# Eight key blocks in one score product, one K buffer refilled in place, and weights parked in one part

## The chip, the cores and the metric

The kernel runs on one core of one Trainium2 chip. TensorE multiplies matrices, VectorE, ScalarE and GpSimd work elementwise, and SyncE (SP) issues most of the DMAs. In the profile's rows they are PE (and PEld for its weight loads), DVE, ACT, POOL and SP. The metric is the device time of one execution in microseconds; lower is better. The median over the runs of the kernel before is compared with that of the changed kernel.

## The reference

A block-sparse attention over 4 batches, 8 heads, 768 positions and 64 dimensions a head, whose output goes through a feed-forward layer with a softplus. In blocks of 32 positions there are 24 blocks. A block of queries sees its neighbours (itself and one on each side), the first and the last block, and three sampled blocks; the first and the last block of queries see all keys.

```python
scores = scale * np.matmul(q, k.transpose(0, 1, 3, 2))
mask = np.abs(blk_i - blk_j) <= 1
mask = mask | (blk_i == 0) | (blk_j == 0) | (blk_i == n_blocks - 1) | (blk_j == n_blocks - 1)
for qb in range(n_blocks):
    for kb in sampled_blocks[qb]:
        mask[qb * block:(qb + 1) * block, kb * block:(kb + 1) * block] = True
scores = np.where(mask, scores, -1000000000.0)
attn = softmax(scores)                       # written out with max, exp, sum
x = (attn @ v) as 3072 tokens of 512
h = x @ w_in                                 # 512 -> 2048, weights are float64
g = np.maximum(h, 0.0) + np.log1p(np.exp(-np.abs(h)))
out = (g @ w_out).astype(np.float32)         # 2048 -> 512
```

## The kernel before

Attention goes by *sets*: for each batch six groups `g` of four query blocks (the last one has two, `ni = 2`), and one set `whole` with the first and last query block against all keys, which stands between groups 4 and 5. Each set is two *units* (`a = 0, 1`, four heads each), 56 units in all: 40 with four blocks, 8 with two, 8 whole. A unit passes through `scores`, `exponents`, `transposes`, `values`; `pieces` starts the scores two units ahead of the values.

For a group, `gather_keys` copies keys from `kT`, the keys of a whole batch in SBUF (1.57 MB), into one of two buffers `kg`: three neighbour blocks for each query block in one VectorE copy (L483), and three sampled blocks each by GpSimd with a register as address (L494). `scores` multiplies those six blocks by 16 matmuls of 192 columns (L585) and the two end blocks straight from `kT` by four more (L591); the eight blocks stand side by side in PSUM, and L599 masks them and takes the row minimum. Whole sets multiply with `kT` (L617). `load_kT` fetches the next batch's keys in four parts into the other of two buffers (pools `kv` and `kv2`), spread over earlier pieces. `load_keys` puts a group on the list of keys to be gathered as soon as its batch's `kT` exists.

The feed-forward layer runs over 16 slices `f` of the 2048 hidden columns and over 8 tiles of 384 tokens, three groups each. Phase 0 does slices 0 to 4 (`EARLY`) between the pieces of attention and parks partial sums in DRAM (`yD`), and the attention's output in `xD`; phase 1 does slices 5 to 15 after attention. One step of the loop over `j` is `hidden` (12 matmuls), a softplus on ScalarE and VectorE, and, three steps later (`LEAD`), `project` (9 matmuls). Each float32 product is made of three products of parts: a value rounded to the matmul's type, `hi`, and the rest, `lo`.

`Weights` converts the float64 weights, 32 halves of 128x512 (`which` 0 and 1 for each `f`), in small steps on ScalarE, VectorE and GpSimd (L153 to L193). It ends in `hi` (L189, ScalarE) and `lo` (L193, VectorE). The 22 halves of `f >= 5` are parked in DRAM, both parts (L198, tiles `wh` and `wt`), and come back after attention through `load_w2` (L893).

Every engine's queue runs in the order in which the program issues; SP's order is that of the code.

Of the kernel before, what the change touches and what calls it, by code (L numbers as in the profile page):

```python
# [37 lines left out]
SPREAD = 2  # L38

# [9 lines left out]
def sparse_attention_ffn(  # L49
# [50 lines left out]
    xp = ctx.enter_context(tc.tile_pool(name="x", bufs=2, side="right"))  # L100
# [10 lines left out]
        (which, f): [dram.tile([P, DM], F32, name=f"wD{x}{which}{f}") for x in range(2)]  # L111
# [7 lines left out]
    class Weights:  # L119
# [62 lines left out]
        def high(self, h):  # L182
            f, which = self.halves[h]
            if f < EARLY:
                W[which, f] = [w1.tile([P, DM], F32R, name=f"w{x}{which}{f}") for x in range(2)]
            else:
                hi = pools["conv"].tile([P, DM], F32R, tag="wh", name=f"wh{which}{f}", bufs=2)
                W[which, f] = [hi, self.t[h].bitcast(F32R)]
            tc.keep_in_program_order(nc.scalar.copy(out=W[which, f][0], in_=self.t[h]))  # L189

        def low(self, h):
            hi, lo = W[self.halves[h][::-1]]
            nc.vector.tensor_tensor(out=lo, in0=self.t[h], in1=hi.bitcast(F32), op=ALU.subtract)  # L193

        def park(self, x, h):
            f, which = self.halves[h]
            if f >= EARLY:
                nc.sync.dma_start(out=wD[which, f][x], in_=W[which, f][x].bitcast(F32))  # L198
# [14 lines left out]
        def done(self):  # L213
            return self.at > 4 * (len(self.halves) - 1) + 14
# [6 lines left out]
    def x_tile(phase, t):  # L221
        X[phase, t] = xp.tile([P, 2, NC, TB], F32R, tag="x", name=f"x{phase}_{t}")
# [247 lines left out]

    def gather_keys(m):
# [4 lines left out]
        def of_block(i):  # L476
# [3 lines left out]
            if i == 0:  # L480
# [6 lines left out]
                tc.keep_in_program_order(ins)  # L487
            (r,) = registers(eng, [2 * g + i // 2])
            for s in range(NR):
# [5 lines left out]
                    out=kd[:, i, NR + s, :], in_=kT[b][:, bass.ds(x, 1), :].rearrange("p n f -> p (n f)")  # L495
# [68 lines left out]
    def scores(n):  # L564
# [6 lines left out]
        if not whole:  # L571
# [6 lines left out]
            for j in range(2):  # L578
                p = 2 * a + j
                cols = slice(p * BLOCK, (p + 1) * BLOCK)  # L580
                for i in range(ni):
                    for r in range(2):
                        half = slice(64 * r, 64 * r + 64)
                        o = ps[r][32 * i : 32 * i + 32, j].rearrange("p (c s) k -> p c s k", c=2)[:, :, 0:NR]
                        nc.tensor.matmul(o, qd[half, p, i, :], kd[half, i, :, cols], start=True, stop=True)  # L585

            for j in range(2):
                p = 2 * a + j
                for r in range(2):
                    half = slice(64 * r, 64 * r + 64)  # L590
                    nc.tensor.matmul(  # L591
                        ps[r][rows, j, NR : NS : NR + 1],
                        qd[half, p, 0:ni, :].rearrange("p i q -> p (i q)"),
                        kT[b][half, 0 : NB : LAST, p * BLOCK : (p + 1) * BLOCK],
                        start=True, stop=True,
                    )
# [163 lines left out]
    def pieces(n):  # L760
# [7 lines left out]
        def score_piece():  # L768
# [3 lines left out]
            if s < len(units):  # L772
                scores(s)
                if scored is not None:
                    load_keys(scored + 2)

        def value_piece():
# [10 lines left out]
            b, i = divmod(n, len(units) // B)  # L788
# [71 lines left out]
    kv2 = ExitStack()  # L860
    owed = 0.0

    def convert():
# [5 lines left out]
        while owed >= 1 and not weights.done():  # L869
            weights.tick()  # L870
            owed -= 1
            if weights.at == 4 * weights.extra + 2:
                extractx.close()
                pools["kv2"] = kv2.enter_context(tc.tile_pool(name="kv2", bufs=1))
# [85 lines left out]
```

## Time and profile before

| | |
|---|---|
| median of 3 runs | 853.09 us (847.7 to 854.35) |
| profiled execution | 850.83 us, span 848.8 us |
| TensorE / its weight loads busy | 811.8 us (96%) / 683.7 us (81%) |
| VectorE / ScalarE / GpSimd busy | 582.0 us (69%) / 486.2 us (57%) / 219.4 us (26%) |
| DMA | 142.30 MB, mean 168 GB/s |
| granted TensorE clock, mean | 0.975 |

The span runs from the first to the last instruction; the execution's own time has about 2 us around it. A row of a timeline reads: start in us, duration in us, engine, line, operation, tiles as out<-in, shape, count; in brackets the idle time before it and what ended it. In a group's row stand the number of instructions, the busy time with the mean duration in ns, and the idle time before them with what ended it.

### The profile page before, as it was taken

The numbers are of one execution on the slowest core, as the hardware profiler recorded it, in microseconds if no ns is written. First come the engines' busy times: TensorE is split into PE (matmuls) and PEld (weight loads), VectorE is DVE, ScalarE is ACT, GpSimd is POOL, SyncE is SP. The second block draws the span as 40 slices with busy tenths as digits, with TensorE's granted clock in tenths as the row PEclk, the third lists the DMA queues.
The fourth block names the chain that finished last, engine by engine and source line by source line (L and its number), as shares of the span: only waits on it lengthen the run. The fifth ranks groups of instructions, "written<-read, shape, count | busy, mean of one in ns | idle before, by whom it ended". The sixth has DMA issues, their size and how long they took to land.

```text
span 848.8 us, 22274 instructions
## 1 busy us (share of the span) xinstructions
PE 811.8 (96%) x8492; PEld 683.7 (81%) x8492; DVE 582.0 (69%) x1473; ACT 486.2 (57%) x1167; POOL 219.4 (26%) x389
## 2 busy tenths in 40 slices
PE   8779899999999899999999999999999999999998
PEld 7657677767778677787789999999999999999996
DVE  4587997787888778877655556556565656565564
ACT  3776776667776667666655544444444444444443
POOL 6582855652545625553000000000000000000000
PEclk9797999999999999998999999999999999999999
DMA  8778598686897877965529923112222203030011
GB/s 254 232 216 310 184 238 273 202 281 198 232 304 237 291 234 203 303 192 189 175 82 379 396 87 112 37 75 75 75 75 75 74 26 125 1 124 27 24 52 38
DMA packets 55323, 142.30 MB, mean 168 GB/s; under 512 B 6256, under 2 KB 6384, under 8 KB 53168
## 3 DMA queue, kind: packets, MB, share of 16 engines
q1 hardware_dynamic: 49216, 122.37, 44.2%
q0 software_dynamic: 5712, 17.57, 7.0%
q8 instruction: 67, 1.10, 0.6%
q10 hardware_dynamic: 288, 0.93, 0.3%
q14 instruction: 40, 0.33, 0.1%
HBM read 104.14 MB, written 36.70 MB: 166 GB/s over the span
## 4 chain that ended last, share of the span: by engine, by line
PE 73%; DVE 10%; ACT 9%; DMA 3%; issue 3%; another core or an unknown queue 1%; SPq 0%; DVEq 0%; ACTq 0%
PE o L291 10%; PE o L292 10%; PE o L293 10%; PE h L235 10%; PE h L236 9%; PE h L237 9%; ACT pr L649 5%; PE x L692 4%; PE s L585 4%; PE t L662 3%; PE s L591 2%; DMA vg<-in_v_dram 2%; PE y L737 1%; ACT pt L669 1%; DVE pr L624 1%
## 5 line engine op out<-in xcount | busy, mean ns | idle before, releaser
L235 PE MATMUL h<-x,w 128*128 128x384 f32 x512 | 176.9, 346 | 1.7 <-DVE nmax L624 1.0
L236 PE MATMUL h<-x,w 128*128 128x384 f32 x512 | 173.1, 338 | 0.0
L237 PE MATMUL h<-x,w 128*128 128x384 f32 x512 | 172.5, 337 | 0.0
L246 DVE TENSOR_SCALAR u<-e 128x384 f32<-128x384 f32 x128 | 49.6, 388 | 168.2 <-ACT e L240 168.1
L291 PE MATMUL o<-w,gh 128*128 128x512 f32 x384 | 156.3, 407 | 0.0
L293 PE MATMUL o<-w,gl 128*128 128x512 f32 x384 | 154.1, 401 | 0.0
L292 PE MATMUL o<-w,gh 128*128 128x512 f32 x384 | 153.7, 400 | 0.0
L649 ACT ACTIVATE pr<-pr,nmax 128x256 f32<-128x256 f32 (+2 forms) x208 | 110.3, 532 | 64.7 <-DVE nmax L599 42.3
L239 ACT ACTIVATE e<-h 128x384 f32<-128x384 f32 x128 | 62.8, 490 | 144.0 <-PE h L237 142.1
L263 ACT CAST gh<-u 128x384 fp32r<-128x384 f32 x128 | 65.7, 513 | 80.7 <-PE o L292 80.6
L235 PEld LDWEIGHTS h<-x,w 128*128 128x128 f32 x512 | 96.7, 189 | 10.5 <-DVE nmax L624 3.1
L550 POOL DMA_INDIRECT vg<-in_v_dram,ix x88 | 88.5, 1005 | 60.8 <-PE x L692 31.5
L494 POOL COPY kg<-kT 128x128 f32 x252 | 85.4, 384 | 59.1 <-PE s L585 53.1
L236 PEld LDWEIGHTS h<-x,w 128*128 128x128 f32 x512 | 96.9, 189 | 4.0
L237 PEld LDWEIGHTS h<-x,w 128*128 128x128 f32 x512 | 96.7, 189 | 0.0
L599 DVE CUSTOM_DVE_ANT_1 pr<-s,mask 128x256 f32<-128x256 f32 (+1 forms) x192 | 69.7, 417 | 28.6 <-PE s L591 16.4
L293 PEld LDWEIGHTS o<-w,gl 128*128 128x128 f32 x384 | 73.2, 191 | 17.5
L292 PEld LDWEIGHTS o<-w,gh 128*128 128x128 f32 x384 | 73.3, 191 | 13.5 <-issue 0.6
L291 PEld LDWEIGHTS o<-w,gh 128*128 128x128 f32 x384 | 73.1, 190 | 13.5 <-issue 0.4
L254 ACT ACTIVATE u<-u 128x384 f32<-128x384 f32 x128 | 67.0, 523 | 24.9 <-DVE e L248 24.9
L269 DVE TENSOR_TENSOR gl<-u,gh 128x384 fp32r<-128x384 f32 x128 | 73.7, 576 | 5.6 <-ACT gh L263 5.6
L248 DVE SCALAR_TENSOR_TENSOR e<-u,e 128x384 f32<-128x384 f32 x128 | 73.0, 570 | 3.9
(81 smaller groups left out, 1147.9 us busy)
## 6 DMA issues: line engine op xcount, KB each, us to landing
vg<-in_v_dram SPq DMA_DIRECT2D x19, 768.0 KB
xD<-x SPq DMA_DIRECT2D x8, 1536.0 KB
x<-xD SPq DMA_DIRECT2D x8, 1536.0 KB
w<-wD SPq DMA_DIRECT2D x44, 256.0 KB
raw<-in_w_in_dram SPq DMA_DIRECT2D x16, 512.0 KB
raw<-in_w_out_dram SPq DMA_DIRECT2D x16, 512.0 KB
qc<-in_q_dram SPq DMA_DIRECT2D x24, 256.0 KB
vg<-in_v_dram SPq DMA_DIRECT2D x12, 512.0 KB
```

The lines of the kernel that those rows point to most:

```text
L235: nc.tensor.matmul(ph, wh[:, cols], hi[:, c], start=(c == 0), stop=False)
L236: nc.tensor.matmul(ph, wh[:, cols], lo[:, c], start=False, stop=False)
L237: nc.tensor.matmul(ph, wl[:, cols], hi[:, c], start=False, stop=(c == NC - 1))
L248: nc.vector.scalar_tensor_tensor(out=e, in0=u, scalar=-1.0, in1=e, op0=ALU.add, op1=ALU.subtract)
L269: nc.vector.tensor_tensor(out=gl, in0=l, in1=G[n].bitcast(F32), op=ALU.subtract)
L291: nc.tensor.matmul(po[m], gh[:, cols], wh, start=first, stop=False)
L292: nc.tensor.matmul(po[m], gh[:, cols], wl, start=False, stop=False)
L293: nc.tensor.matmul(po[m], gl[:, cols], wh, start=False, stop=last)
L494: copy(out=kd[:, i, NR + s, :], in_=kT[b][:, bass.ds(x, 1), :].rearrange("p n f -> p (n f)"))
L550: nc.gpsimd.indirect_dma_start(out=vd[0 : 3 * BLOCK, 1, i, :], out_offset=None, in_=v, in_offset=bass.IndirectOffsetOnAxis(ap=ix[:, b, 4 * ...
L599: nc.vector.tensor_tensor_reduce(out=pr[r][rows, j], in0=ps[r][rows, j], in1=mask[rows, g].unsqueeze(2).to_broadcast([ni * BLOCK, NS, BLOCK]),
L649: nc.scalar.activation(x, x, AF.Exp, bias=nmax[rows, r, j : j + 1], scale=-1.0, accum_out=rs[rows, h : h + 1])
```

## The change

Three things are changed together.

1. `kg` gets eight slots for each query block instead of six. `end_keys` copies the first and the last key block into slots 3 and 7, for the first two groups of a batch (the slots are not overwritten by the later groups); on GpSimd, but for the first two groups of the program on VectorE and ScalarE. A unit's scores are then 16 matmuls of 256 columns, and the product straight from `kT` is gone.
2. There is one `kT` buffer. The next batch's four parts are loaded in `score_piece` right behind the scores of the whole set's second unit, the last reader of `kT`, and the gathering of the next batch's first groups is started there. The space of the second buffer goes to one of the two tiles `x` (pool `x2`).
3. A late weight half is parked as the one float32 that `assemble` leaves, eight ticks (`PARK`) after its first step. `high` and `low` are left out for it. `load_w2` loads it into the `lo` tile, and `split_w2` makes the two parts: a ScalarE copy for `hi`, and a GpSimd subtraction in place for `lo`, for two halves a step ahead of their use.

```diff
-    kg = [ac.tile([P, NI, 2 * NR, NP * BLOCK], F32, name=f"kg{n}") for n in range(2)]
+    kg = [ac.tile([P, NI, NS, NP * BLOCK], F32, name=f"kg{n}") for n in range(2)]
...
-            kT[b] = (pools["kv2"] if b % 2 else kv).tile([P, NB, NP * BLOCK], F32, tag="kT", name=f"kT{b}")
+            kT[b] = kv.tile([P, NB, NP * BLOCK], F32, tag="kT", name=f"kT{b}")
...
+    def end_keys(m, copies):
+        for copy, slot, blkno in zip(copies, (NR, 2 * NR + 1), (0, LAST)):
+            copy(
+                out=kg[m % 2][:, :, slot, :],
+                in_=kT[order[m][0]][:, blkno : blkno + 1, :].to_broadcast([P, NI, NP * BLOCK]),
+            )
...
+                if m % NG < 2:
+                    first = nc.vector.tensor_copy if m == 0 else nc.scalar.copy
+                    end_keys(m, (first, nc.scalar.copy) if m < 2 else 2 * (nc.gpsimd.tensor_copy,))
...
-                        o = ps[r][32 * i : 32 * i + 32, j].rearrange("p (c s) k -> p c s k", c=2)[:, :, 0:NR]
-                        nc.tensor.matmul(o, qd[half, p, i, :], kd[half, i, :, cols], start=True, stop=True)
...
-                    nc.tensor.matmul(
-                        ps[r][rows, j, NR : NS : NR + 1],
-                        qd[half, p, 0:ni, :].rearrange("p i q -> p (i q)"),
-                        kT[b][half, 0 : NB : LAST, p * BLOCK : (p + 1) * BLOCK],
-                        start=True, stop=True,
-                    )
+                        nc.tensor.matmul(
+                            ps[r][32 * i : 32 * i + 32, j], qd[half, p, i, :], kd[half, i, :, cols],
+                            start=True, stop=True,
+                        )
...
+                if whole and a == NA - 1 and b + 1 < B:
+                    gathered(key_work, place[b, g])
+                    for n_ in range(4):
+                        load_kT(b + 1, n_)
+                    load_keys()
...
-            if b == 0 and i in (6, 7):
-                load_kT(1, 2 * i - 12)
-                load_kT(1, 2 * i - 11)
-            elif i < 4 and 0 < b < B - 1:
-                load_kT(b + 1, i)
...
+        def park(self, h):
+            f, which = self.halves[h]
+            if f >= EARLY:
+                nc.sync.dma_start(out=wD[which, f], in_=self.t[h])
...
-                (lambda h: self.park(0, h), 12), (lambda h: self.park(1, h), 14),
-                (self.load, 6 - 4 * self.bufs),
+                (self.park, PARK), (self.load, 6 - 4 * self.bufs),
...
-            for x in range(2):
-                nc.sync.dma_start(out=W[which, f][x].bitcast(F32), in_=wD[which, f][x])
+            nc.sync.dma_start(out=W[which, f][1].bitcast(F32), in_=wD[which, f])
+
+    def split_w2(f, which):
+        hi, lo = W[which, f]
+        nc.scalar.copy(out=hi, in_=lo.bitcast(F32))
+        nc.gpsimd.tensor_tensor(out=lo, in0=lo.bitcast(F32), in1=hi.bitcast(F32), op=ALU.subtract)
...
+        for which in range(2):
+            f = EARLY + j + 3 - SECOND - LEAD * which
+            if EARLY <= f < NF:
+                split_w2(f, which)
```

Where the instructions stand on three engines at the boundary to the third batch: first TensorE, the end of that batch's first unit's scores (`s` the scores in PSUM, `o` the output of `project`), before and then after.

```order
L585 MATMUL s_0_3563<-kg_202,qc_0_3083 32x2x96
L585 MATMUL s_1_3564<-kg_202,qc_0_3083 32x2x96
L591 MATMUL s_0_3563<-kT_2141,qc_0_3083 128x2x32
L591 MATMUL s_1_3564<-kT_2141,qc_0_3083 128x2x32
L291 MATMUL o_0_2895<-w_2094,gh_3329 128x512
```

```order
L597 MATMUL s_0_3435<-kg_180,qc_0_2959 32x256
L597 MATMUL s_1_3436<-kg_180,qc_0_2959 32x256
L293 MATMUL o_0_2782<-w_2020,gh_3208 128x512
```

Of each kind the last two are shown. The sixteen products stay, each a third wider, and the products from `kT` behind them are gone.

SP's queue around the same boundary, before and then after (`vg` values, `qc` queries, `raw` weights as they come, `wD` parked weights).

```order
L758 DMA xD_88<-x_2_2371 128x3072
L525 DMA vg_197<-in_v_dram 128x2x512 x3
L441 DMA qc_0_3083<-in_q_dram 128x512
L198 DMA wD_124<-wh_2969 128x512
L198 DMA wD_125<-wt_2409 128x512
L146 DMA raw_3201<-in_w_out_dram 128x512
L532 DMA vg_198<-in_v_dram 96x2x512
```

```order
L762 DMA xD_88<-x_2_2285 128x3072
L538 DMA vg_175<-in_v_dram 128x2x512 x3
L443 DMA qc_0_2959<-in_q_dram 128x512
L201 DMA wD_122<-wt_2521 128x512
L148 DMA raw_3066<-in_w_out_dram 128x512
L427 DMA kT_3124<-in_k_dram 128x768 x4
L545 DMA vg_176<-in_v_dram 96x2x512
```

One parking write stands where two stood, and the four parts of the keys, which were issued much earlier, now stand here, behind the values of the whole set.

VectorE behind the whole set's scores (L630, L634 the last of them; `xs` and `sums` belong to the normalising, `pt` to the transposes, `wt` to the weights), before and then after.

```order
L630 TENSOR_TENSOR nmax_3240<-nmax_3240 128x1 x2
L722 TENSOR_TENSOR xs_3301<-x_3167,sums_2907 128x512
L720 TENSOR_SCALAR sums_3158<-sums_3158 128x4
L721 RECIPROCAL sums_3158<-sums_3158 128x4
L667 COPY pt_4_3313<-t_4_3312 128x512
L163 TENSOR_SCALAR wt_3299<-wt_3299 128x512
```

```order
L634 TENSOR_TENSOR nmax_3103<-nmax_3103 128x1 x2
L726 TENSOR_TENSOR xs_3177<-x_3033,sums_2794 128x512
L493 COPY kg_180<-kT_3124 128x4x384
L671 COPY pt_4_3189<-t_4_3188 128x512
L165 TENSOR_SCALAR wt_3175<-wt_3175 128x512
L724 TENSOR_SCALAR sums_3024<-sums_3024 128x4
```

The copy of the third batch's first neighbour blocks, which stood some forty rows earlier, behind the scores of group 4, now stands here, ahead of the copy of the transposes.

More of the change, by code (lines that the diff above doesn't have):

```diff
@@ L38 @@
 SPREAD = 2
+PARK = 8
 WARM = 50
@@ L99, in sparse_attention_ffn @@
     ps_x = ctx.enter_context(tc.tile_pool(name="ps_x", bufs=1, space=PSUM))
-    xp = ctx.enter_context(tc.tile_pool(name="x", bufs=2, side="right"))
+    xp = ctx.enter_context(tc.tile_pool(name="x", bufs=1, side="right"))
     w1 = ctx.enter_context(tc.tile_pool(name="w1", bufs=1, side="right"))
@@ L110, in sparse_attention_ffn @@
     wD = {
-        (which, f): [dram.tile([P, DM], F32, name=f"wD{x}{which}{f}") for x in range(2)]
+        (which, f): dram.tile([P, DM], F32, name=f"wD{which}{f}")
         for f in range(EARLY, NF) for which in range(2)
@@ L183, in high @@
             f, which = self.halves[h]
[L184 to L188, printed above, removed]
+            if f >= EARLY:
+                return
+            W[which, f] = [w1.tile([P, DM], F32R, name=f"w{x}{which}{f}") for x in range(2)]
             tc.keep_in_program_order(nc.scalar.copy(out=W[which, f][0], in_=self.t[h]))
         def low(self, h):
-            hi, lo = W[self.halves[h][::-1]]
-            nc.vector.tensor_tensor(out=lo, in0=self.t[h], in1=hi.bitcast(F32), op=ALU.subtract)
-        def park(self, x, h):
             f, which = self.halves[h]
             if f >= EARLY:
-                nc.sync.dma_start(out=wD[which, f][x], in_=W[which, f][x].bitcast(F32))
+                return
+            hi, lo = W[which, f]
+            nc.vector.tensor_tensor(out=lo, in0=self.t[h], in1=hi.bitcast(F32), op=ALU.subtract)
+        def park(self, h):
+            f, which = self.halves[h]
+            if f >= EARLY:
+                nc.sync.dma_start(out=wD[which, f], in_=self.t[h])
         def tick(self):
             for stage, at in (
-                (lambda h: self.park(0, h), 12), (lambda h: self.park(1, h), 14),
-                (self.load, 6 - 4 * self.bufs),
+                (self.park, PARK), (self.load, 6 - 4 * self.bufs),
                 (self.low, 12), (self.high, 10),
@@ L213, in done @@
         def done(self):
-            return self.at > 4 * (len(self.halves) - 1) + 14
+            return self.at > 4 * (len(self.halves) - 1) + 12
     X, E, U, L, G, po = {}, {}, {}, {}, {}, {}
@@ L221, in x_tile @@
     def x_tile(phase, t):
-        X[phase, t] = xp.tile([P, 2, NC, TB], F32R, tag="x", name=f"x{phase}_{t}")
+        X[phase, t] = (pools["x2"] if t % 2 else xp).tile([P, 2, NC, TB], F32R, tag="x", name=f"x{phase}_{t}")
     def load_x(t):
@@ L494, in of_block @@
                 copy(
-                    out=kd[:, i, NR + s, :], in_=kT[b][:, bass.ds(x, 1), :].rearrange("p n f -> p (n f)")
+                    out=kd[:, i, 1 + NR + s, :], in_=kT[b][:, bass.ds(x, 1), :].rearrange("p n f -> p (n f)")
                 )
@@ L775, in score_piece @@
                     load_keys(scored + 2)
+                m, a = units[s]
+                b, g, whole = sets[m]
+                if whole and a == NA - 1 and b + 1 < B:
[3 more added lines that the diff above has]
+                    load_keys()
         def value_piece():
@@ L873, in convert @@
                 extractx.close()
-                pools["kv2"] = kv2.enter_context(tc.tile_pool(name="kv2", bufs=1))
+                pools["x2"] = ctx.enter_context(tc.tile_pool(name="x2", bufs=1))
     while done < needs[0]:
@@ L915, in sparse_attention_ffn @@
             actx.close()
-            kv2.close()
             pools["w2"] = ctx.enter_context(tc.tile_pool(name="w2", bufs=1, side="right"))
```

7 lines of the change are left out of this document (1 added, 6 removed).

## The prediction, made before the changed kernel was run

> **What bounds the kernel now.** I read the page first: the busy times and the shares of the chain that ended last.
>
> ```profile
> PE 811.8 (96%) x8492; PEld 683.7 (81%) x8492; DVE 582.0 (69%) x1473; ACT 486.2 (57%) x1167; POOL 219.4 (26%) x389
> PE 73%; DVE 10%; ACT 9%; DMA 3%; issue 3%; another core or an unknown queue 1%; SPq 0%; DVEq 0%; ACTq 0%
> core 0: 848.8 us, clock 0.975
> ```
>
> TensorE is busy 96% of the span and carries 73% of the chain. What shortens its queue counts, though the quarter of the chain that other engines carry says that not all of it comes back. A busy TensorE need not be one at its peak, so I cut the span into stages at the token tiles and at the end of attention (columns: span, busy PE, PEld, DVE, ACT and POOL with their counts, granted clock, DMA share, GB/s).
>
> ```profile
> 0.00:104.00 104.00, 87.62 (x1490) 67.89 (x1494) 74.03 (x239) 67.94 (x172) 66.14 (x131) 0.90 0.77 239
> 104.00:224.00 120.00, 112.80 (x1725) 88.01 (x1721) 97.50 (x266) 81.76 (x222) 60.31 (x100) 0.96 0.77 231
> 224.00:333.00 109.00, 103.28 (x1641) 81.94 (x1639) 87.60 (x244) 76.68 (x203) 55.16 (x96) 0.98 0.82 254
> 333.00:444.00 111.00, 107.50 (x1650) 85.26 (x1649) 81.13 (x230) 72.35 (x191) 37.78 (x63) 0.97 0.62 197
> 444.00:849.00 405.00, 400.62 (x1995) 360.58 (x1994) 241.73 (x498) 187.43 (x381) 0.00 (x0) 1.00 0.28 99
> ```
>
> Attention (the first four rows, 444 us) is a pipeline of four engines, all 60 to 95% busy. The second phase (405 us) is TensorE alone at clock 1.00, with GpSimd empty. Its matmuls are not changed, so nothing is to be won there but something could be lost. The chain of waits over 60 to 440 us says how the attention stage divides (cut off by the view itself):
>
> ```profile
> by line: ACT pr L649 8.1%; PE x L692 7.6%; PE s L585 7.1%; issue 6.1%; PE t L662 6.0%; PE h L235 4.2%; PE s L591 4.2%; PE o L291 4.0%; PE o L292 3.7%; PE o L293 3.6%; PE h L236 3.5%; PE h L237 3.4%; DVE pr L624 2.3%; DVE pr L599 2.0%; ACT p
> ```
>
> L591, the product that disappears, has 4.2% of 380 us, 16.0 us. The exponents (ACT, L649) are the largest single line, so scores handed over earlier also help ScalarE.
>
> **The change, part by part.** *Score products.* The timeline of TensorE in one ordinary unit, with start and duration of each run of instructions:
>
> ```profile
> 224.73 0.88 PE L585 MATMUL s<-kg,qc 64*32 64x192 f32 x32
> 225.54 0.66 PE L591 MATMUL s<-kT,qc 64*128 64x64 f32 x8
> 226.13 0.58 PE L692 MATMUL x<-vg,pt 128*32 128x64 f32 x14
> ```
>
> Read starts, not durations, since the matmuls overlap: L585 takes 225.54 − 224.73 = 0.81 us, L591 takes 226.13 − 225.54 = 0.59, together 1.40. The 32 records of L585 are four passes of eight that sit in eight corners of the array:
>
> ```profile
> 224.73 0.39 PE L585 MATMUL s<-kg,qc 64*32 64x192 f32 x8
> ```
>
> The first eight are there within 0.39 us although one of them lasts 0.32, so their starts lie within some 0.07 us: the eight run side by side, and 0.81 / 4 = 0.20 us is a pass, with the last pass's drain in it. How a pass grows from 192 to 256 columns comes from two widths of the same kind of product:
>
> ```profile
> L585 PE MATMUL s<-kg,qc x128: 322/323/347, 224.7 to 246.2; 64*32 64x192 f32 x128
> L617 PE MATMUL s<-kT,qc x128: 482/483/533, 75.1 to 412.7; 64*64 64x384 f32 x128
> ```
>
> (483 − 323) / 192 = 0.83 ns a column, so 64 columns add 0.053 us a pass, 0.21 us a unit. A unit goes from 1.40 to 1.02, 0.38 us less, in 40 units. The last group of a batch holds two blocks only; its end blocks and what follows them:
>
> ```profile
> 98.58 0.45 PE L591 MATMUL s<-kT,qc 64*64 64x64 f32 x8
> 98.95 0.45 PE L706 MATMUL x<-vg,pt 128*64 128x64 f32 x8
> ```
>
> There 98.95 − 98.58 = 0.37 goes, and with half the products at most the same 0.21 is added: 0.16 less, in 8 units. Together 40 × 0.38 + 8 × 0.16 = 16.5 us of TensorE. The matmul count of L591 agrees with the number of units:
>
> ```profile
> L591 PE MATMUL s<-kT,qc 64*128 64x64 f32 x320 | 29.4, 298 | 0.7 <-issue 0.5
> L591 PE MATMUL s<-kT,qc 64*64 64x64 f32 x64 | 3.6, 230 | 0.0
> ```
>
> Of the full units 31 fall after 60 us, which with the 8 small ones is 31 × 0.59 + 8 × 0.45 = 21.9 us of L591. The chain has 16.0 of it, 73%, the same share as PE has of the whole chain. I take 16.5 × 0.73 = **12.0 us**. Bounds: 0, if all of it turns into waiting for ScalarE, and 48 × 0.59 = 28, if the wide product costs what the narrow one did.
>
> If what spaces the 32 products is their issue instead (0.81 us / 32 = 25 ns each), their width costs nothing: 0.59 goes and 0 is added, 0.21 us a unit more. The Trainium skill has such a rule ("TensorE: Matmul & The Clock Gate", section "Back-to-back issue gap"): short matmuls are not issued closer together than about 25 ns. The mean agrees to the nanosecond; the eight starts inside some 0.07 us do not. I keep it as a rival.
>
> *Weights parked as one float32.* For the 22 late halves the cast L189, the subtraction L193 and one of the two parking DMAs leave the attention stage. The groups:
>
> ```profile
> L193 DVE TENSOR_TENSOR wt<-wt,wh 128x512 fp32r<-128x512 f32 x22 | 18.4, 837 | 3.9 <-ACT wh L189 3.7
> L189 ACT CAST wh<-wt 128x512 fp32r<-128x512 f32 x22 | 13.5, 613 | 0.0
> ```
>
> That is 18.4 us off VectorE, 13.5 us off ScalarE and 5.8 MB off DMA (22 × 256 KB). How much stood in the way is asked of the chain over 290 to 305 us:
>
> ```profile
> 296.35 6.60 DMA wD<-wh
> 304.55 0.53 ACT wh L189
> 299.00:304.00 5.00, 5.00 (x90) 4.47 (x89) 2.91 (x11) 4.20 (x10) 0.82 (x1) 1.00 0.99 321
> ```
>
> The chain goes 6.6 us through a parking DMA, but the row of the window below it shows TensorE full all the while, so this is cover more than loss. ScalarE and VectorE were 76 and 87 of 109 us busy: most of what they are spared lies in slack. I take **5 us** (bounds 0 and 31.9 × 0.27 + 3 = 12: the chain's non-PE quarter of what goes, and half of that DMA).
>
> *One K buffer, refilled in place.* At three batch boundaries the 1.57 MB of keys can be fetched only after the last read by the whole-row scores (L617). The nearest rows bound the time that is left until the next batch's first score:
>
> ```profile
> 195.60 0.53 PE L617 MATMUL s<-kT,qc 64*64 64x384 f32 x1
> 216.40 0.35 PE L585 MATMUL s<-kg,qc 64*32 64x192 f32 x1
> 304.86 0.55 PE L617 MATMUL s<-kT,qc 64*64 64x384 f32 x4
> 324.89 0.35 PE L585 MATMUL s<-kg,qc 64*32 64x192 f32 x1
> 186.60:188.60 2.00, 1.60 (x8) 0.38 (x8) 2.00 (x7) 0.52 (x1) 0.91 (x1) 1.00 1.03 386
> 190.60:192.60 2.00, 2.00 (x72) 1.70 (x71) 0.69 (x4) 1.34 (x4) 0.60 (x1) 1.00 0.89 276
> ```
>
> 20.8 and 20.0 us from start to start, of which some 1.5 to 2 are the scores themselves: 18.5 us. The two windows show what a full DMA moves, 276 to 386 GB/s: 4.1 to 5.7 us for the four parts, with some 1.5 us of start 5.6 to 7.2. Then GpSimd makes two copies of the end blocks and twelve of sampled blocks:
>
> ```profile
> L494 POOL COPY kg<-kT 128x128 f32 x252 | 85.4, 384 | 59.1 <-PE s L585 53.1 <-DMA kT<-in_k_dram 3.5 <-DVE nmax L599 1.9
> L180 POOL TENSOR_TENSOR wt<-wt,raw 128x512 int32<-128x512 int32 x32 | 43.0, 1344 | 78.3 <-ACT raw L157 43.8 <-ACT pr L649 11.6 <-ACT os L310 7.9
> ```
>
> An end copy writes four blocks: 1.5 us by four of L494, 1.3 by L180, which has the same 512 columns. The twelve take 4.6 us. Serially 7.2 + 1.5 + 4.6 = 13.3 us (the first end copy runs while later parts land), inside 18.5. VectorE's copy of the neighbour blocks needs only the first part, but now stands in its queue ahead of the transposes' copies and the weight steps, about where it has this gap:
>
> ```profile
> 201.57 0.17 DVE L720 TENSOR_SCALAR sums<-sums 128x4 f32<-128x4 f32 x1 [1.29 <-ACT pr L649]
> ```
>
> First part about 200.3, and 1.29 us idle there anyway. I take 0.5 us a boundary, **+1.5**. Bounds 0, and 3 × 8 = 24 if the DMA queue is behind by the time the keys are asked for.
>
> *Split when they come back.* Each of the 22 halves gets a ScalarE cast and a GpSimd subtraction in the second phase; its loads are halved.
>
> ```profile
> 440.00:460.00 20.00, 20.00 (x102) 17.60 (x101) 11.17 (x24) 10.04 (x22) 0.00 (x0) 1.00 0.78 281
> 460.00:480.00 20.00, 20.00 (x102) 18.08 (x101) 11.60 (x25) 10.10 (x22) 0.00 (x0) 1.00 1.04 396
> ```
>
> Here ScalarE is half idle, VectorE 0.57 busy, and the DMA share, 0.78 to 1.04, falls by half: the cast is hidden. A GpSimd subtraction on 128x512 is priced by L180's 1344 ns. It touches VectorE, as a weight step beside L180 shows:
>
> ```profile
> 90.00 1.72 DVE L163 TENSOR_SCALAR wt<-wt 128x512 f32<-128x512 f32 x1
> 90.10 1.32 POOL L180 TENSOR_TENSOR wt<-wt,raw 128x512 int32<-128x512 int32 x1
> L163 DVE TENSOR_SCALAR wt<-wt 128x512 f32<-128x512 f32 x32 | 16.9, 530 | 8.7 <-ACT wt L153 6.8 <-issue 1.5
> ```
>
> 1.72 us instead of the mean 0.53: such an instruction waits out the GpSimd one. In the second phase 22 × 1.34 = 29 us could lock VectorE. A step there is 12 + 9 matmuls, so 102 matmuls in 20 us make a step of 4.1 us, in which VectorE has 0.43 × 4.1 = 1.8 us free; the loop deals out two halves a step, over 11 to 14 steps with 20 to 25 us of that slack, and the output products run three steps behind. I take **+3** (bounds 0 and 29; what the slack leaves over is 4 to 9). The Trainium skill ("GPSIMD Engine Reference", Specifications) has GpSimd and VectorE share an SBUF interface; the trace agrees with the 1.72.
>
> *Start.* The end copies of the first two groups lie on ScalarE and VectorE. The first window leaves TensorE 16 us idle at the loads, which I take to cover them: 0 (bounds 0 and 1.5, the GpSimd price of one such copy).
>
> **Sum** on the profiled execution: 850.83 − 12.0 − 5 + 1.5 + 3 = 838. The runs shown have a median of 853.09, 2.3 above that execution, so **840 us**.
>
> **The rivals.** *Greater gain.* All 16.5 us of TensorE come back, 7 from the weights, and the two costs stay at nothing: 853.1 − 16.5 − 7 = 829. For it: 94 to 97% PE in the windows after 104 us. Against: L649 is the chain's first line. *Width for nothing.* If the products are spaced by issue, 48 × 0.21 × 0.73 = 7 us more go: 833. The page's floor on starts leads there by itself.
>
> *Absorbed.* The freed TensorE time turns into waiting for the exponents: only some 5 us of the 12 stay, the rest as summed, near 848. For it: ACT L649 8.1%; against: the same edit spares ScalarE 13.5 us.
>
> *Slower: the keys come late.* With over about 2.5 MB still ahead of the keys in the DMA queue, at 276 GB/s some 9 us, the first part lands that much later; VectorE's copy then stands in front of the transposes' copies, and TensorE starves for 9 − 1.3 = 7.7 us at each of three boundaries: 840 − 1.5 + 23 = 862. 1.5 MB of values (three loads of 128x2x512), the queries, a parking write and 0.5 MB of raw weights are issued just ahead of the keys, 2.5 MB. Against are SP's rows: the last of them left at 188.01, nine microseconds before the keys would be asked for, and SP issued nothing until 198.51.
>
> ```profile
> 188.01 0.06 SPq L146 DMA_DIRECT2D raw<-in_w_out_dram  x1
> 198.51 0.33 SPq L532 DMA_DIRECT2D vg<-in_v_dram  x1
> ```
>
> Nine microseconds drain 2.5 MB at the slower rate, so little should be left by then.
>
> *The split locks VectorE.* The second phase loses 9 to 15 us at its start instead of 3: 846 to 852; with all 29 exposed, 866. The loads' lead speaks for it being hidden, VectorE's two-input instructions, four of them a step, against.
>
> **How the numbers follow.** A measurement of this kernel tells about 1% (8.5 us) from no change: faster is below 844.6, slower above 861.6. Chances: forecast (834 to 846) 0.50, of which 0.08 above 844.6; greater gain 0.15 and width for nothing 0.05; absorbed 0.12, all within 1%; late keys 0.07, slower; split 0.11, of which 0.02 slower. Faster 0.42 + 0.15 + 0.05 = 0.62, same 0.08 + 0.12 + 0.09 = 0.29, slower 0.09. The range takes in the greater gain down to 826 and reaches over the absorbed case and most of the split case, to 854; outside lie the late keys and the far ends of these two.
>
> **What would show it.** In the profile after: an ordinary unit's score products take 1.0 us from start to start (0.8 would speak for spacing by issue). TensorE has no idle time over 2 us behind a batch boundary, and VectorE no wait over 1 us for the keys' DMA. The attention stage ends near 430 us instead of 444, with VectorE and ScalarE 18 and 13 us less busy in it; the second phase takes 405 to 410. I am wrong if the second phase grows by over 6 us, if the boundaries wait, or if TensorE's waits for the exponents grow by what its scores shrink.

## The result: 0.9% slower, and the profile after

Over 13 executions of each on the same chip the kernel before takes 849.94 us and the changed one 858.28 us. The ratio is 1.0091, with a 95% interval of 1.0069 to 1.0113. The profiled execution of the changed kernel has a span of 857.2 us.

The page of the changed kernel first (busy times, chain by engine), then its stages at the same times as before:

```profile
PE 802.1 (94%) x8108; PEld 662.3 (77%) x8108; DVE 580.3 (68%) x1452; ACT 486.2 (57%) x1170; POOL 261.6 (31%) x423
PE 72%; ACT 10%; DVE 10%; issue 5%; another core or an unknown queue 1%; DMA 0%; POOL 0%; DVEq 0%; ACTq 0%; POOLq 0%
core 0: 857.2 us, clock 0.974
0.00:104.00 104.00, 83.26 (x1386) 61.16 (x1386) 71.27 (x231) 67.48 (x169) 63.21 (x126) 0.92 0.82 235
104.00:224.00 120.00, 108.86 (x1606) 80.81 (x1608) 92.68 (x267) 78.53 (x213) 67.26 (x113) 0.94 0.73 219
224.00:333.00 109.00, 101.98 (x1564) 78.12 (x1559) 81.74 (x235) 73.00 (x200) 59.99 (x101) 0.98 0.78 237
333.00:444.00 111.00, 105.64 (x1574) 81.14 (x1573) 75.84 (x224) 69.82 (x187) 38.53 (x64) 0.98 0.56 178
444.00:849.00 405.00, 398.61 (x1975) 358.43 (x1974) 256.26 (x494) 197.38 (x403) 32.63 (x22) 0.99 0.23 83
```

TensorE is busy 9.7 us less, and yet the span is 8.4 us longer: TensorE stands idle more. Two places account for it: in one the gain is missing, in the other time is lost. To find them I take the start of each feed-forward step (every fourth product of the first line of `hidden`, the first step counted as number 0). By the 42nd step attention is over in both kernels; its first product stands in the timelines of TensorE, before and after:

```profile
476.38 0.34 PE L235 MATMUL h<-x,w 128*128 128x384 f32 x1
```

```profile
475.45 0.34 PE L237 MATMUL h<-x,w 128*128 128x384 f32 x1
```

So all of attention gave 0.9 us where the prediction's sum has 15.5 (12.0 and 5, less 1.5). Four steps later the changed kernel is 8.5 us behind, and stays there to the end. The windows of the changed kernel, and TensorE's timeline in the gap:

```profile
470.00:480.00 10.00, 9.71 (x48) 8.32 (x47) 9.90 (x10) 7.56 (x17) 10.00 (x8) 1.00 0.66 264
480.00:490.00 10.00, 3.90 (x18) 3.05 (x17) 9.90 (x11) 5.13 (x12) 8.50 (x6) 0.88 0.07 26
490.00:500.00 10.00, 10.00 (x41) 8.95 (x41) 5.74 (x12) 3.53 (x8) 0.00 (x0) 0.78 0.38 131
484.96 0.50 PE L293 MATMUL o<-w,gh 128*128 128x512 f32 x1 [2.46 <-ACT os L312]
489.57 0.80 PE L293 MATMUL o<-w,gh 128*128 128x512 f32 x1 [3.65 <-DVE os L312]
```

TensorE is busy 3.9 us of 10, while VectorE is full (9.90) and GpSimd too. TensorE waits for the output tile of phase 0 to be copied out of PSUM (L312), which stands in VectorE's and ScalarE's queues behind softplus work that is late. GpSimd and VectorE at that time, and VectorE again once GpSimd has finished:

```profile
467.45 21.05 POOL L903 TENSOR_TENSOR w<-w,w 128x512 fp32r<-128x512 f32 x14 [4.04 <-ACT w L902]
475.33 1.53 DVE L250 SCALAR_TENSOR_TENSOR e<-u,e 128x384 f32<-128x384 f32 x1
476.89 0.56 DVE L251 SCALAR_TENSOR_TENSOR e<-h,e 128x384 f32<-128x384 f32 x1
477.37 1.07 DVE L271 TENSOR_TENSOR gl<-u,gh 128x384 fp32r<-128x384 f32 x1
478.36 1.65 DVE L261 TENSOR_TENSOR u<-u,e 128x384 f32<-128x384 f32 x1
479.93 1.45 DVE L248 TENSOR_SCALAR u<-e 128x384 f32<-128x384 f32 x1
497.02 0.56 DVE L250 SCALAR_TENSOR_TENSOR e<-u,e 128x384 f32<-128x384 f32 x1
498.55 0.55 DVE L261 TENSOR_TENSOR u<-u,e 128x384 f32<-128x384 f32 x1
```

Fourteen subtractions of the split run without a pause for 21 us, 1.5 us each. Beside them L250 takes 1.53 instead of 0.56 and L261 1.65 instead of 0.55, while L251, which reads `h` in PSUM, keeps its 0.56. The five together take 6.1 us from one L250 to the next (475.33 to 481.41), against 4.2 us for TensorE's step. VectorE loses 1.9 us a step, until the store of a tile has to wait for it.

In attention the new score product does what the sum said. TensorE's timeline of the changed kernel:

```profile
227.11 1.09 PE L597 MATMUL s<-kg,qc 64*32 64x256 f32 x32
228.13 1.09 PE L696 MATMUL x<-vg,pt 128*32 128x64 f32 x32
```

228.13 − 227.11 = 1.02 us a unit, the number forecast. What took it back is in TensorE's groups over 14 to 446 us (busy, mean ns, then idle before and its cause), before and after:

```profile
L692 PE MATMUL x<-vg,pt 128*32 128x64 f32 x2816 | 62.1, 226 | 10.5 <-issue 9.0 <-DMA qc<-in_q_dram 1.1 <-ACT pt L669 0.2
```

```profile
L696 PE MATMUL x<-vg,pt 128*32 128x64 f32 x2816 | 64.8, 228 | 18.1 <-issue 15.7 <-ACT pt L673 2.2
L710 PE MATMUL x<-vg,pt 128*64 128x64 f32 x384 | 14.6, 225 | 2.8 <-issue 2.7
```

"issue" means that TensorE waited for nothing that the profile shows. One such stretch of the changed kernel, TensorE and then GpSimd:

```profile
46.70 0.86 PE L696 MATMUL x<-vg,pt 128*32 128x64 f32 x43
47.72 0.31 PE L696 MATMUL x<-vg,pt 128*32 128x64 f32 x4 [0.16 <-issue]
48.47 0.31 PE L696 MATMUL x<-vg,pt 128*32 128x64 f32 x3 [0.43 <-issue]
49.24 0.22 PE L696 MATMUL x<-vg,pt 128*32 128x64 f32 x1 [0.46 <-issue]
49.96 0.22 PE L696 MATMUL x<-vg,pt 128*32 128x64 f32 x1 [0.51 <-issue]
47.66 0.91 POOL L563 DMA_INDIRECT vg<-in_v_dram,ix  x1 [0.30 <-issue]
48.88 0.91 POOL L563 DMA_INDIRECT vg<-in_v_dram,ix  x1 [0.30 <-issue]
```

43 value products start within a microsecond, and then one to four every 0.7 to 0.8 us, while GpSimd issues indirect DMAs. I sum the gaps of over 0.5 us between starts within runs of equal products on gathered keys or values, with 0.1 us taken off each. They make 16.5 us before (20 gaps) and 27.4 us after (35 gaps); 16.0 and 24.5 of these lie less than 0.2 us from an indirect DMA. Some of the gaps are waits for another engine. Those put down to "issue" are 17 before and 31 after, 11.1 and 22.2 us, so that nearly all the growth is theirs.

The same shows when TensorE's whole time up to the 42nd step is dealt out, each product counted from its start to the start of the next. The score products take 107.5 us before and 93.6 after, the value products 80.8 and 94.0: what the scores gave, the values took back.

### The profile page after: what moved, and what is told of

Its sections match the earlier page's. It is cut to its first block, busy times and chain, and to the rows that moved or that the text cites. A ratio compares the mean times of both kernels' runs of the same rounds, so it can differ in the third digit from the quotient of the medians.

```text
span 857.2 us, 21456 instructions
## 1 busy us (share of the span) xinstructions
PE 802.1 (94%) x8108; PEld 662.3 (77%) x8108; DVE 580.3 (68%) x1452; ACT 486.2 (57%) x1170; POOL 261.6 (31%) x423
## 4 chain that ended last, share of the span: by engine, by line
PE 72%; ACT 10%; DVE 10%; issue 5%; another core or an unknown queue 1%; DMA 0%; POOL 0%; DVEq 0%; ACTq 0%; POOLq 0%
PE h L237 10%; PE o L293 10%; PE o L295 9%; PE o L294 9%; PE h L238 9%; PE h L239 9%; ACT pr L653 5%; PE s L597 4%; PE x L696 4%; PE t L666 4%; DVE e L250 2%; PE warm L827 2%; DVE u L248 2%; PE y L741 1%; ACT pt L673 1%
## 5 line engine op out<-in xcount | busy, mean ns | idle before, releaser
L248 DVE TENSOR_SCALAR u<-e 128x384 f32<-128x384 f32 x128 | 53.8, 420 | 162.3 <-ACT e L242 162.3
L241 ACT ACTIVATE e<-h 128x384 f32<-128x384 f32 x128 | 62.6, 489 | 133.4 <-PE h L239 133.2
L563 POOL DMA_INDIRECT vg<-in_v_dram,ix x88 | 86.7, 986 | 61.0 <-PE x L696 35.0
L603 DVE CUSTOM_DVE_ANT_1 pr<-s,mask 128x256 f32<-128x256 f32 (+1 forms) x192 | 69.9, 417 | 35.5 <-remote 18.5
L696 PE MATMUL x<-vg,pt 128*32 128x64 f32 x2816 | 64.8, 228 | 18.1 <-issue 15.7
L250 DVE SCALAR_TENSOR_TENSOR e<-u,e 128x384 f32<-128x384 f32 x128 | 78.5, 613 | 3.8
```

The lines of the kernel that those rows point to most:

```text
L248: nc.vector.tensor_scalar_add(out=u, in0=e, scalar1=1.0)
L250: nc.vector.scalar_tensor_tensor(out=e, in0=u, scalar=-1.0, in1=e, op0=ALU.add, op1=ALU.subtract)
L563: nc.gpsimd.indirect_dma_start(out=vd[0 : 3 * BLOCK, 1, i, :], out_offset=None, in_=v, in_offset=bass.IndirectOffsetOnAxis(ap=ix[:, b, 4 * ...
L696: nc.tensor.matmul(xq[rows, h * D : (h + 1) * D], pt[r, 2 * j + c][:, rows], vd[:, c, i, h * D : (h + 1) * D], start=(c == 0), stop=(c == 1),)
```

## The experiments

Two theories came out of this: GpSimd's subtractions lock VectorE (hold its instructions up for as long as they last) at the entry to the second phase, and GpSimd's indirect DMAs make TensorE pause in attention. The runs went to several chips, and chips differ: on four of them the kernel before takes 833 to 835 us, on one 851, as on the first. I call the four fast chips and the other two slow ones. Each of the five later chips was used at one time only, so the difference may also belong to the time. Each ratio below is against the kernel before on the same chip; it comes from all the runs and need not be the ratio of the two medians shown.

| kernel | chip (before, us) | time, us | ratio to before, 95% |
|---|---|---|---|
| changed | 849.9 | 858.3 | 1.0091 (1.0069 to 1.0113) |
| changed | 834.5 | 829.7 | 0.9956 (0.9934 to 0.9978) |
| split on VectorE | 833.0 | 821.7 | 0.9869 (0.9838 to 0.9900) |
| split on VectorE | 834.5 | 821.6 | 0.9865 (0.9815 to 0.9916) |
| split on VectorE | 834.6 | 822.3 | 0.9891 (0.9855 to 0.9928) |
| split on VectorE | 834.3 | 822.5 | 0.9868 (0.9838 to 0.9899) |
| scores and K buffer alone | 833.0 | 827.1 | 0.9948 (0.9917 to 0.9980) |
| parking alone, split on VectorE | 833.0 | 824.8 | 0.9891 (0.9862 to 0.9920) |
| half the split on GpSimd | 850.8 | 852.9 | 1.0040 (1.0010 to 1.0070) |
| split on VectorE, idle subtractions on GpSimd | 850.8 | 864.6 | 1.0138 (1.0065 to 1.0212) |

**The split on VectorE.**

```diff
-        nc.gpsimd.tensor_tensor(out=lo, in0=lo.bitcast(F32), in1=hi.bitcast(F32), op=ALU.subtract)
+        nc.vector.tensor_tensor(out=lo, in0=lo.bitcast(F32), in1=hi.bitcast(F32), op=ALU.subtract)
```

> The changed kernel with the 22 subtractions of the split on VectorE instead of GpSimd; nothing else differs. Theory (GpSimd's subtractions lock VectorE at the start of the second phase): the stall of TensorE between the 42nd and the 46th step, 9.3 us in the profile after, goes; VectorE has 22 x 0.6 = 13 us more of its own in some 30 us of slack. Time about 850, 8 to 9 us below the changed kernel, attention ending where it did. Rival (the loads or ScalarE's casts are late): the stall stays and the time is near 858.

Measured 0.9869 of before. Forty microseconds from about the 40th step on, in this kernel:

```profile
438.00:478.00 40.00, 40.00 (x203) 36.31 (x202) 30.79 (x63) 24.74 (x52) 0.00 (x0) 1.00 0.33 126
```

TensorE is full with VectorE at 30.8 of 40. The stall is gone; the absolute time was missed since the chip was a fast one. On one chip, beside the changed kernel itself:

> The changed kernel, unchanged, on the same chip as the other three. Theory (two separate causes): on a chip where the kernel before takes 833 the 9 us at the start of the second phase remain and attention keeps a gain of about 11, so 0.995 to 1.0 of before; where it takes 850, 1.009 again, with 27 us of pauses. Rival (the lock of VectorE alone): the same ratio on any chip.

> The changed kernel with the split's subtractions on VectorE, again, beside the changed kernel itself. Theory (lock of VectorE): 8 to 9 us less than the changed kernel on any chip, with the same end of attention. Rival: the 1.3% of the first experiment is that chip's; then on a slower chip it is no faster than the changed kernel.

829.7 against 821.6 us: 8.1 us, as expected. The same forty microseconds of the changed kernel on that chip:

```profile
438.00:478.00 40.00, 33.60 (x157) 29.43 (x157) 32.19 (x43) 22.69 (x48) 21.05 (x14) 0.91 0.35 132
```

The stall is there with its 21.05 us of GpSimd. The rival "the same ratio on any chip" falls: the changed kernel is 0.4% faster than before here.

**Half of the split, and subtractions that nobody reads.** These two ran on a chip where before takes 850.8 us.

```diff
-        nc.gpsimd.tensor_tensor(out=lo, in0=lo.bitcast(F32), ...)
+        (nc.vector if which else nc.gpsimd).tensor_tensor(out=lo, in0=lo.bitcast(F32), ...)
```

> The changed kernel with 11 of the 22 subtractions of the split on GpSimd (those of the input weights) and 11 on VectorE. Theory (a GpSimd subtraction holds VectorE for its 1.5 us, and TensorE stalls only where that exceeds VectorE's slack): 11 x 1.5 + 11 x 0.6 = 23 us over some 7 to 10 steps with 1.8 us of slack each and three steps of lag; the stall falls from 9 us to 0 to 3, time 0.987 to 0.990 of before. Rival (GpSimd's result comes too late for TensorE, whatever VectorE does): the stall stays above 6 us.

```diff
+        nc.vector.tensor_tensor(out=lo, in0=lo.bitcast(F32), in1=hi.bitcast(F32), op=ALU.subtract)
+        idle = gp.tile([P, DM], F32, tag="idle", name=f"idle{which}{f}", bufs=1)
+        nc.gpsimd.tensor_tensor(out=idle, in0=hi.bitcast(F32), in1=hi.bitcast(F32), op=ALU.subtract)
```

> The changed kernel with the split on VectorE, and 22 subtractions of the same size on GpSimd beside it, whose results nobody reads. Theory (lock of VectorE): the stall at the start of the second phase is back, 9 us or more, since VectorE now has the split to do as well; time near 0.996 to 1.005 of before. Rival (TensorE waited for GpSimd's results): no stall, time as with the split on VectorE, 0.987.

The windows of the two, half the split first:

```profile
466.00:506.00 40.00, 37.38 (x186) 32.93 (x185) 31.87 (x53) 24.01 (x50) 8.78 (x7) 1.00 0.40 147
```

```profile
471.00:511.00 40.00, 30.29 (x131) 25.91 (x131) 37.55 (x49) 20.03 (x42) 21.12 (x17) 0.87 0.39 144
```

From the 40th to the 46th step takes 25.2 us when nothing stalls. By the starts of those steps it takes 467.1 to 501.7 = 34.6 in the changed kernel on the first chip (stall 9.4), 466.3 to 495.0 = 28.7 with half the split on GpSimd (3.5), 438.0 to 463.2 = 25.2 with none (0), and 471.1 to 510.4 = 39.3 with the idle ones added (14.1). The idle subtractions stall TensorE more than the real ones did, though no instruction waits for their results; VectorE has the 22 real ones to do besides. So it is the lock of VectorE, and half as many subtractions cost well under half of the stall, as they would if only what exceeds VectorE's slack counts. The half split's 3.5 us lie just above the 0 to 3 expected. Both ratios, 1.0040 and 1.0138, lie above what was expected; the half split's was worked out from a fast chip.

**The parts of attention alone**, on the fast chip where before takes 833.0 us. First the changed kernel's scores and K buffer with the two-part parking as before (of its edit only the load is shown), then the kernel before with the new parking and the split on VectorE:

```diff
-            nc.sync.dma_start(out=W[which, f][1].bitcast(F32), in_=wD[which, f])
+            for x in range(2):
+                nc.sync.dma_start(out=W[which, f][x].bitcast(F32), in_=wD[which, f][x])
...
```

> The changed kernel with the old two-part parking: eight-slot scores and the single K buffer stay, nothing is split in the second phase. Theory (in attention the shorter score products are eaten by stalls of TensorE, the parking gives little): attention ends within 3 us of the changed kernel's 441, the second phase is as before, time 849 to 853. Rival (the leaner parking is worth 5 us, as the prediction had it): attention ends 5 us later than in the changed kernel, time 855.

> The kernel before with the one-part parking alone, split on ScalarE and VectorE; scores and K buffers as before. Prediction's term: 5 us faster in attention, time 845. Rival (what is spared lies in slack): attention ends within 1.5 us of before, time 849 to 851.

0.9948 and 0.9891: 4.3 us (1.7 to 6.9) and 9.1 us (6.7 to 11.5). By the medians they are 6.0 and 8.2, and both together, with the split on VectorE, 11.4: the two do not simply add up. The 42nd step of the first, and of the kernel with the new parking as well (split on VectorE), on that chip:

```profile
452.22 0.34 PE L237 MATMUL h<-x,w 128*128 128x384 f32 x1
```

```profile
446.40 0.34 PE L237 MATMUL h<-x,w 128*128 128x384 f32 x1
```

The new parking makes 5.8 us of attention there, so the rival held in the first. In the second the 42nd step starts at 453.44, 7.2 us earlier than in the kernel before on another fast chip (460.67 below), somewhat more than the prediction's term. The absolute times of both expectations were for a slow chip.

**The two kernels on a fast chip, for their profiles.**

> The kernel before, unchanged, for a profile on the same chip as the next three. The first experiments ran on a chip on which it takes 833 us, 17 less than where the change was first measured. Theory (a chip is slow because TensorE pauses inside its runs of value and score products): where it takes 850 again, pauses over 0.5 us inside such runs sum to about 16 us; where it takes 833, to under 10.

Before (42nd step), changed:

```profile
460.67 0.34 PE L235 MATMUL h<-x,w 128*128 128x384 f32 x1
```

```profile
446.22 0.34 PE L237 MATMUL h<-x,w 128*128 128x384 f32 x1
```

Here attention gains 14.5 us. Counted from start to start up to this step, the score products take 110.3 and 97.4 us, and the value products 69.9 and 65.5, where the slow chip has 80.8 and 94.0. TensorE's value products in the two have 2.8 us of "issue" and none that is listed:

```profile
L692 PE MATMUL x<-vg,pt 128*32 128x64 f32 x2816 | 57.6, 228 | 5.8 <-issue 2.8 <-ACT pt L669 2.5 <-DMA vg<-in_v_dram,ix 0.5
```

```profile
L696 PE MATMUL x<-vg,pt 128*32 128x64 f32 x2816 | 56.1, 224 | 4.3 <-ACT pt L673 3.8 <-DMA vg<-in_v_dram,ix 0.4
```

The gaps over 0.5 us sum to 11.7 us before, a little over the 10 expected, and 9.4 after; about half lie beside an indirect DMA, and 3.1 and 3.2 us of them are put down to "issue".

**Without indirect DMAs.** One plain DMA a set, of fixed blocks, in place of up to four indirect ones of the sampled blocks.

```diff
-            nc.gpsimd.indirect_dma_start(out=vd[0 : 3 * BLOCK, 1, i, :], out_offset=None, in_=v, ...)
+        nc.sync.dma_start(
+            out=vd[0 : 3 * BLOCK, 1, 0:ni],
+            in_=overlapping(v, b * S + (20 - 4 * g) * BLOCK if g else b * S + 16 * BLOCK, ni, 3 * BLOCK))
```

> As the changed kernel with the split on VectorE, but the values of the sampled blocks are not gathered by 88 indirect DMAs of GpSimd: one plain DMA a set loads fixed blocks of the same size instead, so the output is that of other blocks. Theory (TensorE is starved of instructions while GpSimd issues an indirect DMA: 24.5 of the 27.4 us of pauses over 0.5 us inside runs of score and value products lie beside one): these pauses fall under 5 us and attention ends 15 to 25 us earlier than in the changed kernel, time 825 to 835. Rival (the pauses come from instruction fetching or DMA load in general, the nearness is chance): the pauses stay at 15 us or more, and time gains under 8 us over the kernel with the split on VectorE.

> As the kernel above, with one plain DMA of fixed blocks a set in place of the 88 indirect DMAs (the output is that of other blocks). On the first chip, where pauses are few, it gave nothing. Theory (indirect DMAs starve TensorE, on a chip that shows pauses): where the changed kernel has 27 us of pauses they fall under 5 and this one is 10 us or more faster than the kernel above; where pauses are few, no difference. Rival: pauses stay at 15 us or more on a slow chip.

On fast chips 0.9865 (0.9803 to 0.9927) and 0.9900 (0.9855 to 0.9944): nothing beyond the split on VectorE. The gaps of the first sum to 10.0 us, as with indirect DMAs on that chip (9.9). The theory in its first form fell there: on a fast chip GpSimd's 88 us of issuing cost no more than the plain DMAs in their place. Then on the chip where before takes 850.8:

> The kernel before again, for its profile on this chip. On a chip where it takes about 834: attention (to the 42nd step) until 461 and pauses of 10 to 12 us in runs of score and value products; where it takes 850: 476 and 16 us or more.

> The changed kernel with the split on VectorE and plain DMAs of fixed blocks instead of the 88 indirect ones (the output is that of other blocks). On a chip where before takes 834 it gave nothing. Theory (indirect DMAs starve TensorE where a chip is slow): on such a chip no pauses and attention over 10 us shorter than that of the other two changed kernels here. Rival: no difference there either.

The first steps after attention of before, half the split, and this kernel, all on that chip:

```profile
473.95 0.34 PE L235 MATMUL h<-x,w 128*128 128x384 f32 x1
```

```profile
474.73 0.34 PE L237 MATMUL h<-x,w 128*128 128x384 f32 x1
```

```profile
448.85 0.34 PE L237 MATMUL h<-x,w 128*128 128x384 f32 x1
L690 PE MATMUL x<-vg,pt 128*32 128x64 f32 x2816 | 61.4, 228 | 9.0 <-ACT pt L667 5.3 <-issue 2.4 <-ACT u L256 1.2
```

Attention is 25.9 us shorter without indirect DMAs, the execution took 823.0 us, as on a fast chip, and the stretches of "issue" in the value products are 2.4 us. From start to start the value products take 71.7 us where the half split has 92.3. Pauses do not vanish: the gaps sum to 11.8 us, 9.1 of them "issue". With indirect DMAs this chip repeats the first one: gaps of 17.7 us before and 26.6 us with the change (half split), 16.6 and 22.5 beside an indirect DMA; before, the "issue" gaps come at nearly the same times as on the first chip (near 38, 51, 62, 138 and 158 us). The kernel with plain DMAs was run once there; the 42nd step of the same attention with indirect DMAs lies within 3.2 us in five profiles on fast chips (445.3 to 448.5). A last set and a pair went to fast chips again:

> The kernel before with one plain DMA of fixed blocks a set in place of the 88 indirect DMAs (the output is that of other blocks). Theory (indirect DMAs issued by GpSimd pause TensorE on some chips, and the change's shorter products only make more pauses there): on a chip where before takes 850 this one falls to 830 to 836, attention's 42nd step near 461; where before takes 834 it stays within 6 us of it. Rival (the pauses belong to the changed kernel's denser products alone): no gain over before on any chip.

> As the kernel above with plain DMAs of fixed blocks (the output is that of other blocks), beside the first kernel of this set, so that the change's worth in attention is read without indirect DMAs. Theory: attention's 42nd step 10 to 14 us earlier than in the kernel before with fixed blocks, on any chip, time 821 to 826. Rival (the change gains nothing in attention even so): within 4 us of it.

> The kernel before with one plain DMA of fixed blocks a set in place of the 88 indirect DMAs (the output is that of other blocks). Where before takes 834 it took 836. On a chip where before takes 850, theory (the indirect DMAs pause TensorE there): 830 to 838, 0.975 to 0.985 of before. Rival (the pauses harm only the changed kernel): 848 or more.

> The changed kernel with the split's subtractions on VectorE, hoped to run on a slow chip, where it has not been. Theory: there only the stall at the second phase goes and attention is no shorter than before's: 0.998 to 1.002 of before. On a fast chip 0.987 again. Rival (attention does gain there, the earlier profiles were chance): 0.987 on a slow chip too.

> The changed kernel with the split's subtractions on VectorE. Where before takes 834 it took 0.987 to 0.989 of it. On a chip where before takes 850, theory (attention's gain is eaten by pauses there, the second phase's stall is gone): 0.998 to 1.002 of before. Rival (attention gains there as well): 0.987.

Before with plain DMAs takes 836.4 and 835.8 us (1.0028, interval 1.0002 to 1.0055, and 1.0020, 1.0002 to 1.0037), the changed kernel with them and the split on VectorE 821.7. So on a fast chip the change, so split, is worth 14.7 us without any gathering by indirect DMAs; its 42nd step starts 15.7 us earlier, where 10 to 14 were expected. The split on VectorE gave 0.9891 and 0.9868 there. What the kernel before would gain on a slow chip, and what the split on VectorE gives there, is left open: these runs met fast chips.

**Register-addressed DMAs of SyncE**, an attempt at a kernel that is fast on both kinds of chip:

```diff
-            nc.gpsimd.indirect_dma_start(out=vd[0 : 3 * BLOCK, 1, i, :], ...)
...
+                nc.sync.dma_start(out=vd[s_ * BLOCK : (s_ + 1) * BLOCK, 1, i, :],
+                    in_=v[b * S : (b + 1) * S].rearrange("(n p) f -> p n f", p=BLOCK)[:, bass.ds(x, 1), :].rearrange("p n f -> p (n f)"))
```

> The changed kernel with the split on VectorE, and the sampled blocks' values fetched by SyncE with plain DMAs at addresses from registers, three to a query block, instead of GpSimd's indirect DMAs; the output is the reference's. Theory (pauses come from the indirect DMAs): on any chip about the time of the kernel with fixed blocks, 820 to 828, so 0.965 to 0.975 of before on a slow chip and 0.985 to 0.992 on a fast one. Rival: SyncE's 264 further DMAs in its one queue come late, the values wait, and it is slower than the kernel with the split on VectorE.

878.1 us, 1.0563 of before: the rival held. SyncE's timeline:

```profile
210.84 5.95 SPq L570 DMA_DIRECT2D vg<-in_v_dram  x6
225.47 4.04 SPq L570 DMA_DIRECT2D vg<-in_v_dram  x6
```

Six of them hold SyncE's queue for 4 to 6 us, with all other loads behind them.

## Why the prediction was wrong

The step that failed first is the split: +3 was taken, with bounds 0 and 29; it measured 9.4 in the profile and 8.1 us between two kernels on one chip. The rival that the split locks VectorE had the right mechanism and price (9 to 15 us) and was given 0.11. The working set 29 us of lock against 20 to 25 us of slack over 11 to 14 steps. The runs show why that mean was no guide: GpSimd did not take two a step but 14 in a row, 21 us, and over that stretch VectorE was 1.9 us a step short. They could follow so closely because ScalarE's casts, on which they wait, do not come two a step either:

```profile
L902 ACT CAST w<-w x22: 602/610/622, 451.1 to 480.6; 128x512 fp32r<-128x512 f32 x22
```

All 22 start within 29.5 us, seven steps of 4.2 us and not 11 to 14, and five of them stand in ScalarE's queue between the L241 of one step at 472.27 and the next at 478.35. The 1.72 us row of the prediction was the evidence of the lock; it was used for the bound and not for the value taken. The Trainium skill ("GPSIMD Engine Reference", Specifications) names this contention, and here its size is L261's 1.65 against 0.55 us.

The second is attention, right on one kind of chip and wrong on the other. The score unit came out at 1.02 us as worked out; the rival of width for nothing is refuted by 0.81 growing to 1.02. The floor of the Trainium skill ("TensorE: Matmul & The Clock Gate", section "Back-to-back issue gap") did not set the pace here: the mean rose from 25 to 32 ns a product. On fast chips attention gained 14.5 us of the 15.5 in the sum in one pair of profiles, and 9 to 11 by the four ratios of the split on VectorE, which has no stall after it. How that is shared between the terms is less sure: scores and K buffer alone gave 4.3 us (1.7 to 6.9) where 10.5 stood, parking alone 9.1 where 5 stood, but parking on top of the new scores 5.8. On the first chip all of attention gained 0.9. The chain's share of 73% was taken to say that removed TensorE time comes back. What it missed is the idle time that had no releaser: 9.0 us of "issue" stood in the trace of before, in the value products, and it grew by 9.4 us with L710's. The absorbed case named the exponents; the pauses took their place: over 14 to 446 us TensorE's waits for ScalarE grew from 6.4 to 8.9 us only.

At the batch boundaries VectorE hardly waits for the keys, as forecast, but GpSimd does. The waits of both on the keys over 14 to 440 us in the changed kernel (us, times, longest):

```profile
POOL kg L476 <- DMA kT<-in_k_dram: 7.9, 3, 5.2
DVE kg L493 <- DMA kT<-in_k_dram: 1.6, 3, 0.8
```

VectorE's 1.6 us over three places stand where the sum has +1.5. GpSimd's queue, ahead of the gathers of values, was not looked at, and behind the first boundary the same lock of VectorE seems to stand. VectorE, GpSimd and TensorE there, in the changed kernel on a fast chip:

```profile
84.96 6.10 DVE L261 TENSOR_TENSOR u<-u,e 128x384 f32<-128x384 f32 x1
85.11 4.29 POOL L507 COPY kg<-kT 128x128 f32 x18
96.37 0.66 PE L666 MATMUL t<-ident,pr 64*128 64x64 f32 x4 [6.93 <-DVE nmax L603]
```

One addition of VectorE lasts 6.10 us beside eighteen copies of keys in a row and the weight step of GpSimd behind them, and TensorE then waits 6.93 us for VectorE's row minima. In the kernel before on that chip the same addition takes 1.44 us and the wait is 1.49. The 6.93 are there in all five profiles of the changed kernel's attention on fast chips and with the two-part parking, and not with the new parking alone (1.49): they come with the scores and the K buffer. On the first chip the wait is 2.53 us, against 2.06 before. So on fast chips the +1.5 was too small, and TensorE's idle time of over 2 us behind a boundary, which the prediction named as a sign against it, is there. No run gives the keys' copies another order, so what this costs in the end is not shown. The rival of late keys did not happen as it was described: VectorE waits 0.8 us for them at most. Over the four attention windows VectorE is 18.7 us less busy (18 forecast) and ScalarE 9.9 (13), by the sums of their columns. But attention did not end near 430, and the second phase grew by over 6 us, which the prediction named as what would make it wrong.

That the same change is 0.9% slower on one chip and 0.4% faster on another is shown. That indirect DMAs pause TensorE on the slow kind rests on one execution without them; why they do so on that kind only stays open.

## What to carry to other kernels

An elementwise operation with two inputs on an idle GpSimd is not free where VectorE works beside it: price it at its full duration on VectorE, and look at how many can come in a row rather than at the mean per step. A long run of GpSimd's copies seems to do the same. Idle time of the bounding engine that has no releaser is a cost of its own, and a change that makes an instruction-dense stretch shorter need not shorten it. Before a per cent is credited to a change, run it on more than one chip.

## What was not expected of the hardware

After the stall TensorE's granted clock is 0.78 in 490 to 500 us, and its twelve products from 489.57 on take 4.65 us where they take 2.45 otherwise: the 2.2 us between, a quarter of the 9.4, go with the lower clock. On two chips TensorE starts one to four products every 0.7 to 0.8 us while GpSimd issues an indirect DMA. The "issue" gaps beside such a DMA make 10 to 11 us before and 18 to 21 with the change there, and at most 3 on the four others.
